# The rounded part of g written by GpSimd or by a casting transfer, and batch 3's squared rows added by GpSimd, in a fused channel attention and ELU feed-forward kernel

## The chip, the cores and the metric

The kernel runs on one core of a Trainium2 chip. The core has five engines that run at the same time, each with a queue of its own that it works through in order: TensorE (PE in the profile, with its weight loads as PEld), VectorE (DVE), ScalarE (ACT), GpSimd (POOL) and SyncE (SP, which here only starts transfers). Engines wait for one another through semaphores. Transfers run on 16 DMA engines. SBUF is the on-chip memory of 128 partitions, and PSUM is the memory that matmuls write to. The metric is the device time of one launch in microseconds; a time here is the median of its runs.

## The reference

Four batches (B) of 6080 rows (N) and 256 channels (C) go through a channel attention and then, as 24320 tokens, through a feed-forward layer of width 2048 with ELU:

```python
qn = q / (np.linalg.norm(q, axis=1, keepdims=True) + 1e-06)
kn = k / (np.linalg.norm(k, axis=1, keepdims=True) + 1e-06)
s = kn.transpose(0, 2, 1) @ qn / tau          # 256 x 256 for each batch
s = s - s.max(-1, keepdims=True)
a = np.exp(s)
a /= a.sum(-1, keepdims=True) + 1e-09
x = (v @ a).reshape(B * N, C)
h = x @ w_in                                  # 24320 x 2048
g = np.where(h > 0.0, h, np.exp(np.minimum(h, 0.0)) - 1.0)
out = g @ w_out                               # 24320 x 256
```

q, k, v are float32; the two weight matrices come as float64. The norms run over the 6080 rows.

## The kernel before, in words

The attention matrix of a batch is multiplied into `w_in` first, so that a batch has one matrix `wp` of 256 x 2048 and `h = v @ wp`. The tokens are cut into 12 chunks of 512 or 496 tokens for each batch, 48 chunks in all (`NCH`), and the feed-forward width into 16 blocks of 128 (`FT`). One step is one chunk `c` and one block `f`; there are 768 steps. The first four chunks share 64 steps in an interleaved order; from chunk 4 on, 16 steps in a row belong to one chunk.

Every matmul operand is kept as two parts: `hi`, the float32 value rounded to fp32r, and `lo`, what the rounding took away, also as fp32r. A product is then the sum of three fast matmuls: hi with hi, lo with hi, hi with lo. The helper `split` (L113 to L115) makes the two parts: ACT writes hi with a casting copy (L114) and DVE writes lo with a subtraction (L115).

`take(i)` (L833) issues step i:

- `h_item` (L416): six matmuls (L423, L424, L425, twice) of `wp` and the split chunk of v give `ph` in PSUM.
- `elu` (L428): gives `e`, of 128 x 512 float32 in SBUF. In even blocks ACT takes the exponential (L438), DVE limits it and subtracts one (L439) and takes the maximum with `ph` (L440). In odd blocks ACT does a Relu and an exponential (L434, L435) and DVE one combined instruction (L436). L439 has one input in SBUF; L436 and L440 have one in SBUF and one in PSUM.
- `split_g` (L443) of the step before: hi and lo of `e` go into a tile `g`.
- `out_item` (L455) of step i - 3 (`LAG`): six matmuls (L461, L463, L465, twice) add the product of g and `w_out` to `po`; L461 and L463 read hi, L465 reads lo. Between them stand single matmuls of the next batch's product of k and q (`gram_item`, L203 and L210).

There are three buffers for `e` and four for `g`. An `e` buffer is free again when its lo has been made, a `g` buffer when PE has used it.

Beside the steps run the next batch's rows: 24 groups of two rows in each partition are loaded by SP (`raw`, five buffers), squared by ACT (L181 into the single buffer `sq`), added to `acc` (L182, DVE, 128 x 1024 float32), and split for the gram matmuls (`qk`, L114 and L115). In the last group POOL first clears a part of the buffer (L169). Batch 1's groups run in chunks 4 to 10, batch 2's in chunks 13 to 21, batch 3's in chunks 25 to 33. After them come that batch's norms and softmax (L226 to L315) and its `wp` (L351 to L382), within the two chunks that follow. The chunks of v are split into hi and lo by L404 and L408. Both inputs lie in SBUF in the subtractions of L115 (g, qk) and L408 and in the additions of L182.

The order of PE, DVE and ACT is written out by hand up to step 66. After that a planner orders the instructions of each engine by the order in which they are traced and by the time at which it expects their inputs; `issue_after` keeps the work beside the steps behind the step's elu. The queues of SP and POOL are ordered by the planner as well.

Of the kernel before, what the change touches and what calls it, by code (L numbers as in the profile page):

```python
# [7 lines left out]
F32 = mybir.dt.float32  # L8
# [46 lines left out]
def channel_attention_then_elu_ffn(ctx: ExitStack, tc, q, k, vT, tau, w_in, w_out, outT):  # L55
# [8 lines left out]
    nc = tc.nc  # L64
    B, N, C = q.shape
# [9 lines left out]
    NB = len(sizes)  # L75
    NCH = B * NB
    LAG = 3


    M = 4  # L80
# [32 lines left out]
    def split(hi, lo, src):  # L113
        nc.scalar.copy(hi, src)  # L114
        nc.vector.tensor_sub(lo, src, hi.bitcast(F32))  # L115
# [50 lines left out]
    def load_rows(b, g):  # L166
        raw = work.tile([P, 2, 2, C], F32, tag="raw", bufs=5, name=f"raw_{b}_{g}")
        if 2 * g + 2 > RP:
            nc.gpsimd.memset(raw[:, :, 1, :], 0.0)  # L169
        fill_rows(raw, b, g)  # L170
        if 2 * g + 2 > RP:
            fill_left(raw, b)
        return raw

    def square_rows(raw, acc, first, sq=None):
        if first:
            nc.scalar.activation(acc, raw, AF.Square)
            return
        if sq is None:
            sq = work.tile([P, 2, 2, C], F32, tag="sq", bufs=1, name="sq")  # L180
        x = nc.scalar.activation(sq, raw, AF.Square)  # L181
        return x.ins, nc.vector.tensor_add(acc, acc, sq).ins  # L182

    def new_acc(b):
        return work.tile([P, 2, 2, C], F32, tag="acc", bufs=1, name=f"acc_{b}")

    def new_gram(b):
        return [ps.tile([P, 2, C], F32, tag="gram", bufs=KT, name=f"gram_{b}_{ct}") for ct in range(KT)]

    def split_rows(raw):  # L190
        hl = work.tile([P, 2, 2, 2, C], F32R, tag="qk", bufs=3, name="qk")
        split(hl[:, 0], hl[:, 1], raw)
        return hl

    def gram_item(hl, gram, ct, first, last):

        pg = gram[ct]  # L200
        cs = slice(ct * P, ct * P + P)
        for r in range(2):
            yield nc.tensor.matmul(  # L203
                pg,
                hl[:, 0, 1, r, cs],
                in_turns(hl[:, :, 0, r, :]),
                start=(first and r == 0),
                stop=False,
            )
            yield nc.tensor.matmul(  # L210
                pg[:, 0, :],
                hl[:, 1, 1, r, cs],
                in_turns(hl[:, 0, 0, r, :]),
                start=False,
                stop=(last and r == 1),
            )
# [53 lines left out]
    def norms(parts):  # L270

        pn = ps.tile([P, 2, C], F32, tag="w", bufs=WB, name="pn")
        for x in range(2):
            nc.tensor.matmul(pn[:, 0, :], ones_r, in_turns(parts[:, x, 0, :]), start=(x == 0), stop=(x == 1))
        for ct in range(KT):
            for x in range(2):

                nc.tensor.matmul(
                    pn[:, 1, 2 * ct : 2 * ct + 2],
                    parts[:, x, 1, ct * P : ct * P + P],  # L280
                    ones_r[:, 0:2],
                    start=(x == 0),
                    stop=(x == 1),
                )
        W = C + 2 * KT
        y, ry = (tiny.tile([P, W], F32, tag=x, bufs=1, name=x) for x in ("y", "ry"))
        nm = inverse_norms(y, ry, pn.rearrange("p x c -> p (x c)")[:, 0:W])
        rk = tiny.tile([P, 2 * KT], F32, bufs=2, tag="rk", name="rk")
        nc.vector.tensor_scalar(rk, ry[:, C:W], itau, None, op0=ALU.mult)

        return halves_of_turns(ry[:, 0:C]), rk.rearrange("p (c x) -> p c x", x=2)[:, :, 0], nm
# [26 lines left out]
    def soft_rows(b, gram):  # L318

        a = work.tile([P, KT, C], F32, tag="a", bufs=1, name=f"a_{b}")  # L320
        for ct in range(KT):
            row = halves(a[:, ct])
            nc.scalar.copy(row, halves_of_turns(gram[ct][:, 1, :]))
            nc.vector.tensor_add(row, halves_of_turns(gram[ct][:, 0, :]), row)
            if b == 1:
                nc.vector.tensor_add(a[:, ct], a[:, ct], state["early"][:, ct])
        return a
# [5 lines left out]
    def transpose_a(b, a):  # L333
        pt = ps.tile([P, KT, C], F32, tag="w", bufs=WB, name="pt")
        for jt in range(KT):
            for ct in range(KT):
                nc.tensor.transpose(pt[:, jt, ct * P : ct * P + P], a[:, ct, jt * P : jt * P + P], ident)  # L337
        if b == 0:
            aT = tiny.tile([P, KT, C], F32, tag="early", bufs=1, name=f"aT_{b}")
            for jt in range(KT):  # L340
                nc.scalar.copy(aT[:, jt], pt[:, jt])
            return aT
        aT = work.tile([P, 2, KT, C], F32R, tag="aT", bufs=1, name=f"aT_{b}")
        split(aT[:, 0], aT[:, 1], pt)
        return aT
# [12 lines left out]
    def new_wp(b):  # L358
        return [
            work.tile([P, 2, F], F32R, tag="wp", bufs=2 * KT, name=f"wp_{b}_{ct}") for ct in range(KT)  # L360
        ]
# [23 lines left out]
    def span(c):  # L385

        b, x = divmod(c, NB)
        return b, b * N + sum(sizes[:x]), sizes[x]
# [54 lines left out]
    def split_g(c, e):  # L443
        n = span(c)[2]
        g = work.tile([P, 2, CH], F32R, tag="g", bufs=4, name="g")
        split(g[:, 0, 0:n], g[:, 1, 0:n], e[:, 0:n])
        return g

    def first(c, f):
# [91 lines left out]
    acc = new_acc(0)  # L541
    pg0 = new_gram(0)
    wi64, wo64, vraw, vts = {}, {}, {}, {}
    state = {}
# [141 lines left out]
    def chunk_of(b):  # L686
        return b * NB
# [7 lines left out]
    def at(step, fn, free=False):  # L695
        (loose if free else side).setdefault(step, []).append(fn)
# [72 lines left out]
    def first_group(b):  # L769

        return EARLY if b == 1 else 0

    for b in range(1, B):
        s0 = M * FT if b == 1 else chunk_of(b - 1) * FT + FT
        s1 = chunk_of(b) * FT
        length = s1 - FT - 14 - s0

        g0 = first_group(b)

        def rows(b, g):  # L780
            if g == 0:
                state[b, "acc"], state[b, "gram"] = new_acc(b), new_gram(b)
            raw = state.pop((b, "raw", g))
            square_rows(raw, state[b, "acc"], g == 0)
            if g >= first_group(b):
                state[b, "hl", g] = split_rows(raw)

        def load(b, g):
            if g < NG:
                state[b, "raw", g] = load_rows(b, g)  # L790

        def gram(b, g, ct):
            g0 = first_group(b)
            yield from gram_item(state[b, "hl", g], state[b, "gram"], ct, g == g0, g == NG - 1)

        def soft_norms(b):
            state[b, "norms"] = norms(state[b, "parts"])
            state[b, "rs"] = tiny.tile([P, KT], F32, tag="sums", bufs=2, name="sums")

        def soft_sum(b):  # L800
            state[b, "a"] = soft_rows(b, state[b, "gram"])
            wps[b] = new_wp(b)

        def soft2(b):
            state[b, "aT"] = transpose_a(b, state[b, "a"])

        for g in range(NG):
            x = s0 + length * g // NG
            if g == 0:
                at(x, lambda b=b, g=g: (load(b, g), load(b, g + 1)))  # L810
            at(x + 2, lambda b=b, g=g: (rows(b, g), load(b, g + 2)))
            for ct in range(KT if g >= g0 else 0):
                fine[x + 5 + ct] = gram(b, g, ct)
        x = s1 - FT - 6
        at(x - 6, lambda b=b: state.__setitem__((b, "parts"), fold(state[b, "acc"])))
        at(x - 4, lambda b=b: soft_norms(b))
        at(x - 2, lambda b=b: soft_sum(b))
        for ct in range(KT):
            at(x + ct, lambda b=b, ct=ct: soft_exp(state[b, "a"], *state[b, "norms"], state[b, "rs"], ct))
        at(x + 3, lambda b=b: over_sums(state[b, "rs"]))  # L820
        at(x + 6, lambda b=b: soft2(b))
        x += 6
        for fq in range(FQ):
            at(x + 1 + 3 * fq, lambda b=b, fq=fq: state.__setitem__((b, "wi", fq), split_w_in(fq)))
            for ct in range(KT):
                at(x + 4 + 3 * fq + ct, lambda b=b, fq=fq, ct=ct: wp_item(state[b, "aT"], state[b, "rs"], state[b, "wi", fq], wps[b], ct, fq))
# [6 lines left out]
    def take(i):  # L833
# [5 lines left out]
        if 0 <= i - 1 < len(steps):  # L839
            gs[i - 1] = split_g(steps[i - 1][0], es.pop(i - 1))  # L840
        j = i - LAG
        if j >= 0:
# [16 lines left out]
    done = []  # L859
    for i in range(M * FT + LAG):  # L860
        take(i)
    in_order.close()
    for i in range(M * FT + LAG, len(steps) + LAG):
        take(i)
# [31 lines left out]
```

## Time and profile before

| | |
|---|---|
| median of the two timed runs | 2166.32 us (2165.83 and 2166.81) |
| span of the profiled execution, first to last instruction | 2163.4 us |
| instructions | 27196 |
| DMA | 120.77 MB, 56 GB/s on the mean |
| SP's issues of v, q, k, weights and out | all transfers but one, none by POOL |

The page lists no time of the profiled execution other than its span, so sums are made against the span; the timed runs lie 2.4 and 3.4 us above it. In the views, a row of instructions gives the line, the engine, the operation, what it writes and reads (out<-in), the count, then the busy time in us and the mean duration in ns, and last the idle time of the engine just before them with what ended it. A matmul's duration in the profile is longer than its spacing to the next, since matmuls are pipelined. L numbers are lines of the kernel before.

### The profile page before, as it was taken

Reading aid. Unit: us, or ns where it says so; the run is one execution under the profiler, and the core shown is the slowest. Engines: PE = TensorE matmul, PEld = TensorE weight load, DVE = VectorE, ACT = ScalarE, POOL = GpSimd, SP = SyncE. Lnnn points to the kernel's source line nnn. Section 1 sums busy time; section 2 is a strip of 40 time slices with the busy share of each in tenths; the row PEclk is TensorE's granted clock in tenths of the full one; section 3 lists DMA queues with packets and bytes.
Section 4 is the critical chain, followed back from the end, with each engine's and each line's share of the span. In section 5 each row is a group of like instructions: output and inputs, shape, how many; then the busy total and the mean of one; then the engine's idle time right before and its main releaser. Section 6 shows DMA issues by size and latency. Waiting matters only on the chain.

```text
span 2163.4 us, 27196 instructions
## 1 busy us (share of the span) xinstructions
PE 2158.6 (100%) x10240; PEld 1911.9 (88%) x10240; DVE 1527.0 (71%) x2358; ACT 1469.1 (68%) x2422; POOL 3.3 (0%) x11
## 2 busy tenths in 40 slices
PE   9999999999999999999999999999999999999999
PEld 8888888899888888889988888888998888888998
DVE  7987777778766776776776677667776666666665
ACT  6877777667666666666766666666776666666665
POOL 0000000000000000000000000000000000000000
PEclk9999999999999999999999999999999999999999
DMA  9320222221111111111111112111112000000000
GB/s 357 107 78 30 78 69 68 68 65 49 59 38 50 49 59 49 59 58 46 39 59 39 49 50 68 49 58 49 56 31 67 20 30 27 23 20 11 20 10 20
DMA packets 62532, 120.77 MB, mean 56 GB/s; under 512 B 6208, under 2 KB 16064, under 8 KB 62400
## 3 DMA queue, kind: packets, MB, share of 16 engines
q1 hardware_dynamic: 62256, 118.91, 16.6%
q8 instruction: 80, 1.31, 0.2%
q14 instruction: 52, 0.43, 0.1%
q10 hardware_dynamic: 144, 0.13, 0.0%
HBM read 92.01 MB, written 27.00 MB: 55 GB/s over the span
## 4 chain that ended last, share of the span: by engine, by line
PE 100%; ACT 0%; DVE 0%; issue 0%
PE po L465 15%; PE po L463 15%; PE ph L423 15%; PE po L461 15%; PE ph L424 15%; PE ph L425 15%; PE gram L203 3%; PE gram L549 2%; PE gram L210 1%; PE pw L374 1%; PE pw L373 1%; PE pw L375 1%; PE pe L549 0%; PE pw L370 0%; PE pd L222 0%; PE pt L337 0%
## 5 line engine op out<-in xcount | busy, mean ns | idle before, releaser
L114 ACT CAST g<-e 128x512 fp32r<-128x512 f32 (+1 forms) x768 | 469.6, 611 | 483.5 <-DVE e L440 281.6
L115 DVE TENSOR_TENSOR g<-e,g 128x512 fp32r<-128x512 f32 (+1 forms) x768 | 525.6, 685 | 323.0 <-ACT g L114 295.6
L465 PE MATMUL po<-g,wo 128*128 128x512 f32 (+1 forms) x1536 | 579.3, 377 | 0.0
L463 PE MATMUL po<-g,wo 128*128 128x512 f32 (+1 forms) x1536 | 579.2, 377 | 0.0
L461 PE MATMUL po<-g,wo 128*128 128x512 f32 (+1 forms) x1536 | 578.9, 377 | 0.0
L423 PE MATMUL ph<-vt,wp 128*128 128x512 f32 (+1 forms) x1472 | 555.4, 377 | 0.0
L425 PE MATMUL ph<-vt,wp 128*128 128x512 f32 (+1 forms) x1472 | 554.5, 377 | 0.0
L424 PE MATMUL ph<-vt,wp 128*128 128x512 f32 (+1 forms) x1472 | 554.5, 377 | 0.0
L436 DVE SCALAR_TENSOR_TENSOR e<-e,ph 128x512 f32<-128x512 f32 (+1 forms) x416 | 283.2, 681 | 242.5 <-ACT e L435 241.9
L434 ACT ACTIVATE e<-ph 128x512 f32<-128x512 f32 (+1 forms) x416 | 246.6, 593 | 129.1 <-PE ph L425 114.4
L461 PEld LDWEIGHTS po<-g,wo 128*128 128x128 f32 x1536 | 290.3, 189 | 37.9 <-DVE scr L478 0.2
L463 PEld LDWEIGHTS po<-g,wo 128*128 128x128 f32 x1536 | 290.3, 189 | 37.8
L465 PEld LDWEIGHTS po<-g,wo 128*128 128x128 f32 x1536 | 290.7, 189 | 34.8 <-DVE g L115 0.3
L424 PEld LDWEIGHTS ph<-vt,wp 128*128 128x128 f32 x1472 | 278.2, 189 | 36.2
L425 PEld LDWEIGHTS ph<-vt,wp 128*128 128x128 f32 x1472 | 278.2, 189 | 36.1
L423 PEld LDWEIGHTS ph<-vt,wp 128*128 128x128 f32 x1472 | 278.2, 189 | 36.1
L435 ACT ACTIVATE e<-e 128x512 f32<-128x512 f32 (+1 forms) x416 | 261.3, 628 | 12.6
L440 DVE TENSOR_TENSOR e<-ph,e 128x512 f32<-128x512 f32 (+1 forms) x352 | 240.6, 684 | 10.4
L438 ACT ACTIVATE e<-ph 128x512 f32<-128x512 f32 (+1 forms) x352 | 207.9, 591 | 31.1 <-PE ph L425 29.2
L439 DVE TENSOR_SCALAR e<-e 128x512 f32<-128x512 f32 (+1 forms) x352 | 147.0, 418 | 20.7 <-ACT e L438 20.6
L182 DVE TENSOR_TENSOR acc<-acc,sq 128x1024 f32<-128x1024 f32 x84 | 102.6, 1221 | 12.2 <-ACT sq L181 11.1
L203 PE MATMUL gram<-qk 128*128 128x512 f32 x268 | 101.6, 379 | 0.0
(134 smaller groups left out, 1183.1 us busy)
## 6 DMA issues: line engine op xcount, KB each, us to landing
raw<-in_q_dram SPq DMA_DIRECT2D x76, 256.0 KB, 2.7
raw<-in_k_dram SPq DMA_DIRECT2D x76, 256.0 KB, 3.0
v<-in_v_dram SPq DMA_DIRECT2D x32, 512.0 KB, 3.6
out_dram<-o SPq DMA_DIRECT2D x56, 256.0 KB, 2.1
v<-in_v_dram SPq DMA_DIRECT2D x16, 496.0 KB, 3.5
out_dram<-o SPq DMA_DIRECT2D x31, 248.0 KB, 2.1
wraw<-w_scr SPq DMA_DIRECT2D x12, 512.0 KB, 3.2
room<-in_q_dram SPq DMA_DIRECT2D x16, 256.0 KB, 5.2
```

What stands on the lines that cost most here:

```text
L114: nc.scalar.copy(hi, src)
L115: nc.vector.tensor_sub(lo, src, hi.bitcast(F32))
L423: nc.tensor.matmul(ph[:, 0:n], wp[kt][:, 0, fs], hi, start=(kt == 0), stop=False)
L424: nc.tensor.matmul(ph[:, 0:n], wp[kt][:, 0, fs], lo, start=False, stop=False)
L425: nc.tensor.matmul(ph[:, 0:n], wp[kt][:, 1, fs], hi, start=False, stop=(kt == KT - 1))
L434: nc.scalar.activation(ev, pv, AF.Relu, scale=-1.0)
L435: x = nc.scalar.activation(ev, ev, AF.Exp, scale=-1.0)
L436: y = nc.vector.scalar_tensor_tensor(ev, ev, -1.0, pv, op0=ALU.add, op1=ALU.max)
L440: y = nc.vector.tensor_tensor(ev, pv, ev, op=ALU.max)
L461: nc.tensor.matmul(o, wo[:, f, 0, ds], hi, start=first(c, f), stop=False)
L463: nc.tensor.matmul(o, wo[:, f, 1, ds], hi, start=False, stop=False)
L465: nc.tensor.matmul(o, wo[:, f, 0, ds], lo, start=False, stop=last(c, f))
```

## The change

Three things change.

In chunks 8 to 15 (`POOL_COPIES`) hi is written by GpSimd's copy in place of ScalarE's. In chunks 20 to 27 (`POOL_CASTS`) it is written by a transfer from SBUF to SBUF, started from GpSimd's queue, that casts float32 to fp32r. In the other chunks ScalarE writes it as before. lo stays with VectorE everywhere. The squared rows of batch 3 are added to `acc` by GpSimd; those of batches 1 and 2 stay with VectorE. 128 steps are touched by the copies, 128 by the casts, and 23 additions move.

```diff
+    POOL_COPIES, POOL_CASTS = (8, 16), (20, 28)
...
-    def square_rows(raw, acc, first, sq=None):
+    def square_rows(raw, acc, first, sq=None, adder=nc.vector):
...
         x = nc.scalar.activation(sq, raw, AF.Square)
-        return x.ins, nc.vector.tensor_add(acc, acc, sq).ins
+        return x.ins, adder.tensor_add(acc, acc, sq).ins
...
         g = work.tile([P, 2, CH], F32R, tag="g", bufs=4, name="g")
-        split(g[:, 0, 0:n], g[:, 1, 0:n], e[:, 0:n])
+        hi, lo, src = g[:, 0, 0:n], g[:, 1, 0:n], e[:, 0:n]
+        if POOL_COPIES[0] <= c < POOL_COPIES[1]:
+            nc.gpsimd.tensor_copy(hi, src)
+        elif POOL_CASTS[0] <= c < POOL_CASTS[1]:
+            nc.gpsimd.dma_start(hi, src)
+        else:
+            nc.scalar.copy(hi, src)
+        nc.vector.tensor_sub(lo, src, hi.bitcast(F32))
         return g
...
-            square_rows(raw, state[b, "acc"], g == 0)
+            square_rows(raw, state[b, "acc"], g == 0, None, nc.gpsimd if b == B - 1 else nc.vector)
```

## The prediction, made before the changed kernel was built or run

> **What bounds the kernel now.** I read the page first (busy times, the clock row, the chain that ended last), then the waits, then the stretches in which the changed chunks run, then single instructions in order of time.
>
> ```profile
> span 2163.4 us, 27196 instructions
> ...
> PE 2158.6 (100%) x10240; PEld 1911.9 (88%) x10240; DVE 1527.0 (71%) x2358; ACT 1469.1 (68%) x2422; POOL 3.3 (0%) x11
> ...
> PEclk9999999999999999999999999999999999999999
> ...
> PE 100%; ACT 0%; DVE 0%; issue 0%
> ```
>
> TensorE (PE) is busy for all but 4.8 us of the span, at the full clock, and the chain that ended last is PE alone. So no work taken off ScalarE (ACT) or VectorE (DVE) can shorten the span by more than those 4.8 us, and they lie at its two ends. The change takes no matmul away. It can cost nothing or make PE wait. The question is how much room lies between the moment g is finished and the moment PE needs it. Of all the weight loads of the out product, one waited for g:
>
> ```profile
> PEld po L465 <- DVE g L115: 0.3, 1, 0.3
> ```
>
> The room of an ordinary step shows in the timeline of chunk 9 (start, duration, engine, line):
>
> ```profile
> 504.33 0.67 DVE L440 TENSOR_TENSOR e<-ph,e 128x496 f32<-128x496 f32 x1
> ...
> 505.03 0.61 ACT L114 CAST g<-e 128x496 fp32r<-128x496 f32 x1 [0.18 <-DVE e L440]
> ...
> 505.67 0.67 DVE L115 TENSOR_TENSOR g<-e,g 128x496 fp32r<-128x496 f32 x1 [0.67 <-ACT g L114]
> ...
> 509.74 0.37 PE L461 MATMUL po<-g,wo 128*128 128x496 f32 x1
> ...
> 510.49 0.38 PE L465 MATMUL po<-g,wo 128*128 128x496 f32 x1
> ```
>
> e is ready at 505.00, the rounded part (hi) at 505.64, the rest (lo) at 506.34. PE takes hi at 509.74 and lo at 510.49. Both are 4.1 us early. Where a batch's norms and softmax run, the room is nearly gone; in chunk 10 a lo that ends at 530.90 is loaded at 531.36:
>
> ```profile
> 530.23 0.67 DVE L115 TENSOR_TENSOR g<-e,g 128x496 fp32r<-128x496 f32 x1
> ...
> 531.36 0.19 PEld L465 LDWEIGHTS po<-g,wo 128*128 128x128 f32 x1
> ```
>
> The stretches in question are 418.7 to 778.4 us (chunks 8 to 15, the copies) and 957.7 to 1313.4 us (chunks 20 to 27, the casts). Columns: length, then busy time and count of PE, PEld, DVE, ACT, POOL, clock, DMA share, GB/s.
>
> ```profile
> 418.70:778.40 359.70, 359.70 (x1728) 320.37 (x1728) 257.94 (x402) 245.99 (x409) 0.68 (x1) 1.00 0.16 52
> 957.70:1313.40 355.70, 355.70 (x1703) 316.69 (x1703) 251.03 (x394) 241.30 (x403) 0.73 (x1) 1.00 0.15 48
> ```
>
> PE has no hole in either, and GpSimd (POOL) is idle.
>
> **The change, part 1: 128 copies move from ACT to POOL (chunks 8 to 15).** What ACT loses:
>
> ```profile
> L114 ACT CAST g<-e 128x512 fp32r<-128x512 f32 (+1 forms) x128 | 78.2, 611 | 80.2 <-DVE e L440 42.7 <-DVE e L436 37.3
> ```
>
> These 78.2 us buy nothing, since ACT bounds nothing. What POOL takes for such a copy, before does not show. The nearest rows (mean ns of one):
>
> ```profile
> L169 POOL MEMSET raw<- 128x512 f32 x3 | 2.1, 715 | 1516.7 <-DVE qk L115 1516.7
> L559 POOL MEMSET ragged<- 128x512 f32 x1 | 0.5, 528 | 0.0
> masks.py:199 POOL TENSOR_SCALAR_AFFINE_SELECT ident<-ident 128x128 f32<-128x128 f32 x1 | 0.3, 293 | 0.0
> ```
>
> The lower end is 0.53 us, the undisturbed memset of the same shape. The select, the one POOL row that also reads, gives 4 x 0.293 = 1.17 us for four times the elements. If a casting copy reads and writes in turn instead of together, it is 1.17 + 0.72 = 1.89 us, the upper end. I take 1.85, near the upper end: I count on the slow case of reading, rounding and storing in one pass per element each, and this is the weakest step of the sum. As a delay alone it is harmless: 1.85 - 0.61 = 1.24 us against 4.1.
>
> What matters more is whether POOL and DVE can work at once. The memset ran beside DVE three times; the first:
>
> ```profile
> 457.74 0.41 DVE L439 TENSOR_SCALAR e<-e 128x496 f32<-128x496 f32 x1
> ...
> 457.94 0.68 POOL L169 MEMSET raw<- 128x512 f32 x1 [456.18 <-DVE qk L115]
> ...
> 458.07 0.67 DVE L115 TENSOR_TENSOR g<-e,g 128x496 fp32r<-128x496 f32 x1
> ```
>
> It took 0.68 us where the undisturbed one took 0.53, longer by 0.15, and it had met the last 0.21 us of the tensor_scalar. The subtraction that followed kept its usual 0.67 us beside it. So one kind of DVE instruction (one input, at double rate: 417 ns where two inputs take 682) keeps POOL out, and a write alone does not hinder a subtraction. The copy reads as well as writes. I take it that it and DVE's instructions with two SBUF inputs exclude each other in the same way. The Trainium skill states this (SBUF — State Buffer, "Who interferes with whom"): the two share one pair of ports, a two-input DVE instruction contends with a GpSimd instruction that reads and not with one that only writes, and the second to start waits for the whole first. The three rows agree with both halves they can show; no row shows a POOL read beside DVE, and by the rule the sum below stands, without it part 1 is near nothing.
>
> DVE's instructions in the copies' stretch:
>
> ```profile
> L115 DVE TENSOR_TENSOR g<-e,g 128x512 fp32r<-128x512 f32 (+1 forms) x128 | 87.3, 682 | 57.3 <-ACT g L114 56.0
> L440 DVE TENSOR_TENSOR e<-ph,e 128x512 f32<-128x512 f32 (+1 forms) x64 | 43.6, 681 | 1.8
> L436 DVE SCALAR_TENSOR_TENSOR e<-e,ph 128x496 f32<-128x496 f32 (+1 forms) x64 | 43.3, 677 | 35.7 <-ACT e L435 35.7
> L439 DVE TENSOR_SCALAR e<-e 128x512 f32<-128x512 f32 (+1 forms) x64 | 26.7, 417 | 2.3 <-ACT e L438 2.3
> L182 DVE TENSOR_TENSOR acc<-acc,sq 128x1024 f32<-128x1024 f32 x16 | 19.5, 1221 | 2.2 <-ACT sq L181 2.2
> L115 DVE TENSOR_TENSOR qk<-raw,qk 128x1024 fp32r<-128x1024 f32 x16 | 19.5, 1218 | 1.7 <-ACT qk L114 1.7
> L408 DVE TENSOR_TENSOR vt<-v,vt 128x512 fp32r<-128x512 f32 (+1 forms) x16 | 10.8, 676 | 0.0
> ```
>
> The five groups that have two SBUF inputs or the double rate come to 87.3 + 26.7 + 19.5 + 19.5 + 10.8 = 163.8 us; L436 and L440 have one of their inputs in PSUM and are taken as free of POOL. The copies add 128 x 1.85 = 236.8. Together 400.6 us must pass one after the other in 359.7 us: at least 41 us over. The break-even of a copy is (359.7 - 163.8) / 128 = 1.53 us. Packing will not be perfect: the next copy needs the next e, which DVE makes in L436 or L440 (43.6 + 43.3 = 86.9 us) behind a blocked subtraction in its queue. If half of that finds POOL idle, the excess is 41 + 43 = 84; if DVE and POOL strictly alternate it is 257.9 + 236.8 - 359.7 = 135. I take the middle of 41 and 84: +63 us. Queued behind a blocked subtraction on DVE are the next e, the split of v and qk and so, three steps later, PE.
>
> **Part 2: 128 rounded parts come by a casting transfer (chunks 20 to 27).** ACT loses about as much again, for nothing. POOL issues 128 transfers of 256 KB from SBUF to SBUF. Before has none of these; the nearest by size (KB each, us from issue to landing):
>
> ```profile
> raw<-in_k_dram SPq DMA_DIRECT2D x76, 256.0 KB, 3.0
> out_dram<-o SPq DMA_DIRECT2D x56, 256.0 KB, 2.1
> room<-in_q_dram SPq DMA_DIRECT2D x16, 256.0 KB, 5.2
> ```
>
> So 2.1 us with free queues, 5.2 among the crowd of the start. The DMA engines are 0.15 busy here, so I take 3.0 and 0.5 for POOL's own issue (as long as its memset): 3.5, later than ACT by 2.9. An ordinary step has 4.1 to spare and loses nothing. In batch 2's softmax (chunk 22), where the spare is 0.5 as in chunk 10, a step comes 2.4 late. The lateness moves PE and so gives room to the next: 2.4 at least, 25 if some ten steps each pay in full. I take +10. The subtraction waits for the transfer at the head of DVE's queue, where the next step's e stands behind it; this too fits as long as the transfer takes under two steps (355.7 / 128 = 2.78 each). SP's queue loses and gains nothing; its loads share the DMA engines. The two memsets of POOL (L169 in chunks 8 and 20) now stand among copies and casts; each waits for a free raw buffer, and if put early holds those behind it by up to a step or so: taken as nothing, at most 6 us.
>
> **Part 3: batch 3's additions go to POOL.** DVE loses the 23 of the first row; 8 (second row) fall in the casts' chunks 25 to 27.
>
> ```profile
> L182 DVE TENSOR_TENSOR acc<-acc,sq 128x1024 f32<-128x1024 f32 x23 | 28.1, 1220 | 3.1 <-ACT sq L181 3.1
> ...
> L182 DVE TENSOR_TENSOR acc<-acc,sq 128x1024 f32<-128x1024 f32 x8 | 9.7, 1215 | 0.0
> ```
>
> On POOL such an addition is between the memset's rate (8 x 128 elements, about 1.0 us) and the select's (8 x 0.293 = 2.3). At 2.3 it is hidden by the 4.1 us and by the 17 us between two of them (8 in the 134.8 us of chunks 25 to 27); with that cover gone it is 23 x (2.3 - 1.2) = 25. A cast issued behind one of the eight is up to 2.3 later, 5.8 in all against 4.7 of room: +1 each at worst, half of them: +4.
>
> **Sum.** 63 + 10 + 4 = 77 us on the profiled execution's 2163.4 us of span; the two timed runs lie about 3 us above that span (median 2166.3). 2166.3 + 77 = 2243 us.
>
> **The rivals.** (1) Not slower: the copy is short, or does not exclude DVE. With 1.36 us (select rate plus one 0.19 wait, the memset's 0.72 - 0.53) POOL and DVE need 163.8 + 174 = 338 us of 359.7 and the 4.1 us absorb the rest. Only parts 2 and 3 remain: 2166 to 2185, some 2178. It decides below 1.53 us a copy. For it speaks the select's 1.17, against it that the cast must read, round and write a full stream. The Trainium skill (GPSIMD Engine Reference, section 4.1) calls one-input work on this engine roughly line-rate, which would put the copy under 0.8 us and the sum at this rival's. (2) The casts are the trouble: landings over 4.7 us. e has three buffers and PE runs three steps behind, so each step pays a third of what is over: at 5.2 us 128 x 0.17 = 21, at 7 us 128 x 0.77 = 98, with part 1 small: 2190 to 2270. The rows with free queues speak against it. (3) Faster: PE's 4.8 us of not being busy is all there is, under 2%.
>
> **How the numbers follow.** The forecast's mechanism (POOL and DVE exclude each other and the copy is over 1.53 us) has 0.58, own range 2205 to 2320; rival 1 0.32; rival 2 0.08; faster 0.02. A measurement tells about 2% (43 us) from no change: the forecast is over that except in its lowest part (0.02), rival 2 mostly. So faster 0.02, same 0.35, slower 0.63. The range leaves out the strict alternation with late casts and the exact tie: 2168 to 2315.
>
> **What would show it.** Right: in the copies' stretch POOL's copies take about 1.85 us each, PE has holes that end with L115 (lo) or a copy, the stretch grows from 360 to about 420 us, and DVE's subtractions stand idle behind POOL rather than run longer. Wrong: copies under 1.5 us, or copies and subtractions that overlap in time without loss. For part 2: casts landing in about 3.5 us and the stretch longer by 5 to 20 us only around the softmax; for part 3: no hole in PE after 1360 us. The prediction fails most easily on the copy's duration, next on whether a copy excludes a subtraction.

## The result, and the profile after

The changed kernel takes 2186.39 us (median of two runs, 2184.45 and 2188.34) where the kernel before takes 2166.32: a ratio of 1.0095, with a 95% interval of 1.0078 to 1.0111. The change costs 20 us, under the 2% that count as slower. The forecast was 2243.

The page of the changed kernel (part 1, the chain's shares, the transfers' row: count, KB each, median us from issue to landing):

```profile
span 2182.5 us, 27584 instructions
...
PE 2167.3 (99%) x10240; PEld 1910.4 (88%) x10240; DVE 1528.3 (70%) x2335; ACT 1326.7 (61%) x2166; POOL 220.6 (10%) x290
...
PE 33%; ACT 3%; DVE 3%; issue 1%; DMA 0%; DVEq 0%
...
g<-e POOLq DMA_DIRECT2D x64, 256.0 KB, 2.3
```

The chain that was PE alone now passes through ACT and DVE, and its shares add up to 40%: beyond that it could not be followed back. Stretches by the same steps as before (the windows' columns are those of the prediction: length, busy time and count of PE, PEld, DVE, ACT, POOL, clock, DMA share, GB/s):

```profile
418.70:779.30 360.60, 360.52 (x1728) 320.01 (x1728) 264.38 (x402) 179.09 (x283) 92.98 (x127) 1.00 0.17 52
958.90:1331.20 372.30, 362.76 (x1703) 315.98 (x1702) 243.84 (x388) 171.97 (x275) 85.21 (x134) 1.00 0.43 134
```

The copies' stretch took 359.7 us and takes 360.6, with PE busy throughout. The casts' stretch took 355.7 and takes 372.3: 16.6 of the 19.1 us by which the span grew. What PE's weight loads waited for in the whole run (us in total, times, longest us):

```profile
PEld po L469 <- DMA g<-e: 10.1, 10, 2.5
PEld po L473 <- DVE g L454: 6.4, 14, 1.0
PEld ph L424 <- DVE wp L383: 2.9, 3, 1.2
```

L469 loads hi, L473 lo (L461 and L465 before), L454 is the subtraction, L449 the copy, L451 the cast. PE waits for casts and for what follows a cast on DVE; no row names the copy. The copies' stretch by lines:

```profile
L449 POOL CAST g<-e 128x512 fp32r<-128x512 f32 (+1 forms) x126 | 92.3, 732 | 260.0 <-DVE e L441 122.8 <-DVE e L437 117.0 <-PE po L473 9.9
L454 DVE TENSOR_TENSOR g<-e,g 128x512 fp32r<-128x512 f32 (+1 forms) x128 | 88.0, 688 | 76.9 <-POOL g L449 75.5 <-ACT g L453 1.4
...
L183 DVE TENSOR_TENSOR acc<-acc,sq 128x1024 f32<-128x1024 f32 x16 | 22.5, 1406 | 1.8 <-ACT sq L182 1.7
L116 DVE TENSOR_TENSOR qk<-raw,qk 128x1024 fp32r<-128x1024 f32 x16 | 22.3, 1395 | 0.0
```

A copy takes 0.73 us on the mean, not 1.85. Beside it DVE's long instructions with two SBUF inputs take 1.41 and 1.40 us instead of 1.22 each: something is exclusive, but little.

### The profile page after: what moved, and what is told of

Same layout as the page of the kernel before. It is cut to its first block, busy times and chain, and to the rows that moved or that the text cites. A ratio compares the mean times of both kernels' runs of the same rounds, so it can differ in the third digit from the quotient of the medians.

```text
span 2182.5 us, 27584 instructions
## 1 busy us (share of the span) xinstructions
PE 2167.3 (99%) x10240; PEld 1910.4 (88%) x10240; DVE 1528.3 (70%) x2335; ACT 1326.7 (61%) x2166; POOL 220.6 (10%) x290
## 5 line engine op out<-in xcount | busy, mean ns | idle before, releaser
L454 DVE TENSOR_TENSOR g<-e,g 128x512 fp32r<-128x512 f32 (+1 forms) x768 | 531.6, 693 | 403.2 <-ACT g L453 193.6
L469 PE MATMUL po<-g,wo 128*128 128x512 f32 (+1 forms) x1536 | 580.2, 378 | 6.3 <-DMA g<-e 6.3
L473 PE MATMUL po<-g,wo 128*128 128x512 f32 (+1 forms) x1536 | 581.1, 378 | 1.8 <-DVE g L454 1.4
L453 ACT CAST g<-e 128x512 fp32r<-128x512 f32 (+1 forms) x512 | 313.4, 612 | 352.3 <-DVE e L441 217.6
L437 DVE SCALAR_TENSOR_TENSOR e<-e,ph 128x512 f32<-128x512 f32 (+1 forms) x416 | 283.1, 681 | 172.8 <-ACT e L436 171.7
L469 PEld LDWEIGHTS po<-g,wo 128*128 128x128 f32 x1536 | 290.3, 189 | 47.7 <-DMA g<-e 10.1
L473 PEld LDWEIGHTS po<-g,wo 128*128 128x128 f32 x1536 | 290.8, 189 | 40.9 <-DVE g L454 6.4
L441 DVE TENSOR_TENSOR e<-ph,e 128x512 f32<-128x512 f32 (+1 forms) x352 | 240.7, 684 | 10.3
L440 DVE TENSOR_SCALAR e<-e 128x512 f32<-128x512 f32 (+1 forms) x352 | 147.9, 420 | 20.6 <-ACT e L439 20.1
L449 POOL CAST g<-e 128x496 fp32r<-128x496 f32 (+1 forms) x128 | 93.5, 730 | 673.8 <-ACT e L435 412.4
L116 DVE TENSOR_TENSOR qk<-raw,qk 128x1024 fp32r<-128x1024 f32 x67 | 105.0, 1568 | 18.6 <-ACT qk L115 17.2
```

Of the source, the lines that this page charges most:

```text
L437: y = nc.vector.scalar_tensor_tensor(ev, ev, -1.0, pv, op0=ALU.add, op1=ALU.max)
L441: y = nc.vector.tensor_tensor(ev, pv, ev, op=ALU.max)
L469: nc.tensor.matmul(o, wo[:, f, 0, ds], hi, start=first(c, f), stop=False)
L473: nc.tensor.matmul(o, wo[:, f, 0, ds], lo, start=False, stop=last(c, f))
```

## The experiments

Times are medians, in us. The kernel before took 2165.6 to 2166.0 in every one of these comparisons.

| run | what differs | us | ratio, interval |
|---|---|---|---|
| e1_copies | copies alone | 2166.47 | 1.0004, 0.9994 to 1.0013 |
| e2_casts | casts alone | 2177.56 | 1.0055, 1.0038 to 1.0072 |
| e3_adds | additions alone | 2166.93 | 1.0005, 0.9995 to 1.0014 |
| e11_copies_twice | each copy made twice | 2209.64 | 1.0203, 1.0188 to 1.0219 |
| e4_copies_thrice | each copy made three times | 2251.76 | 1.0398, 1.0382 to 1.0413 |
| e14_twice_later | twice, lo behind the next e | 2168.04 | 1.0011, 1.0001 to 1.0021 |
| e13_thrice_later | three times, lo behind the next e | 2184.68 | 1.0088, 1.0070 to 1.0106 |
| e12_copies_for_casts | additions, and copies in chunks 20 to 27 | 2168.10 | 1.0012, 1.0002 to 1.0021 |
| e5_casts_quiet | casts alone, in chunks 38 to 45 | 2169.41 | 1.0017, 1.0007 to 1.0026 |
| e6_casts_quiet_loads | the same with loads added | 2170.60 | 1.0023, 1.0014 to 1.0033 |
| e10_casts_late_adds | casts, additions only behind them | 2178.14 | 1.0058, 1.0043 to 1.0073 |
| e9_before_lag4 | before, PE four steps behind | 2167.60 | 1.0009, 0.9999 to 1.0018 |
| e7_lag4 | the whole change, four steps | 2180.22 | 1.0066, 1.0051 to 1.0081 |
| e15_lag4_later | e7, lo behind the next e | 2177.45 | 1.0053, 1.0036 to 1.0069 |
| e16_later | the whole change, lo behind the next e | 2190.72 | 1.0113, 1.0097 to 1.0128 |
| e17_lag4_no_adds | e7 without the additions | 2173.97 | 1.0037, 1.0024 to 1.0051 |
| e18_lag4_later_no_adds | e15 without the additions | 2170.66 | 1.0023, 1.0013 to 1.0033 |
| e19_later_no_adds | e16 without the additions | 2177.36 | 1.0053, 1.0038 to 1.0068 |

### One part at a time

```diff
-    POOL_COPIES, POOL_CASTS = (8, 16), (20, 28)
+    POOL_COPIES, POOL_CASTS = (8, 16), (48, 48)   # e1; e2 (48, 48), (20, 28); e3 both (48, 48)
...
-            square_rows(raw, state[b, "acc"], g == 0, None, nc.gpsimd if b == B - 1 else nc.vector)
+            square_rows(raw, state[b, "acc"], g == 0, None, nc.vector)    # e1 and e2
```

> The copies alone (chunks 8 to 15), no casts, batch 3's additions on DVE. Theory A (a copy takes 0.73 us in the mean, under the 1.53 us at which POOL and DVE would fill the stretch, so they are free; the loss lies with the casts): 0 to 2 us over before. Rival B (the exclusion of POOL and DVE makes the loss, in the copies' stretch too, and shows later as a shifted queue): 5 us or more.

> The casts alone (chunks 20 to 27), batch 3's additions on DVE. Theory A (casts that land late because other transfers are in flight): 10 to 15 us over before, the rest of the 19 us of span being casts that stand behind an addition on POOL. Rival B (POOL's additions make the loss): under 5 us. Rival C (the planner's other order of the queues makes it, whatever the casts do): about 17 us, as in the changed kernel.

> Batch 3's additions alone on POOL, ACT makes every rounded part. Theory A: 0 to 2 us over before, since a subtraction that is held for up to 1.8 us has 4.1 us of room. Rival B (the exclusion makes the loss): 5 us or more.

The copies cost 0.5 us, the additions 1.0, neither of them apart from nothing by its interval; the casts cost 11.6. The three make 13.1, the whole change 20.1. So 7 us come only when parts are together, and the term of 63 us is gone.

### Why the copies cost nothing, and when they would

```diff
-            nc.gpsimd.tensor_copy(hi, src)
+            for _ in range(3):                        # e4; range(2) in e11
+                nc.gpsimd.tensor_copy(hi, src)
```

> As the copies alone, but POOL makes each copy three times over, 3 x 0.62 = 1.85 us without waiting, which is the duration that the prediction took. If POOL and DVE really exclude each other as the prediction has it, 163.8 + 128 x 1.85 = 400 us have to pass in 360 us: 40 to 85 us over before. If they only delay each other a little, the added delay of 1.24 us is within the 4.1 us of room: 0 to 5 us over before.

> As the copies alone, but each made twice, 2 x 0.62 = 1.24 us, under the break-even of 1.53 us. If the exclusion of POOL and DVE is what cost 86 us with three copies: 163.8 + 128 x 1.24 = 322 us fit into 360, and the time is 0 to 15 us over before. If it was the delay of the copy (its cost growing by the same amount with each copy): 40 us or more.

A copy that waits for nothing takes 0.62 us, so three hold POOL for about the 1.85 us of the prediction, and they cost 86 us, within the 41 to 135 of its part 1. But two, 1.24 us and under its break-even of 1.53, cost 44: the second copy costs about 43 and the third 42, and no threshold shows. A part of this may be clock: the granted clock of the stretch was 0.97 in e4 and 0.99 in e11, and if matmuls lengthen with it, 359.7 us of them grow by 11 and 4 us, an estimate; how much of that PE would have waited anyway is not separated. The timeline of e11 (start, us, engine, line; x1 is a single copy, x2 the two copies of a step; L455 is the subtraction there):

```profile
654.61 0.62 POOL L450 CAST g<-e 128x512 fp32r<-128x512 f32 x1
...
655.87 0.68 DVE L437 SCALAR_TENSOR_TENSOR e<-e,ph 128x512 f32<-128x512 f32 x1
...
656.68 1.29 POOL L450 CAST g<-e 128x512 fp32r<-128x512 f32 x2 [1.46 <-DVE e L437]
658.01 0.69 DVE L455 TENSOR_TENSOR g<-e,g 128x512 fp32r<-128x512 f32 x1 [1.46 <-POOL g L450]
...
658.62 0.42 DVE L440 TENSOR_SCALAR e<-e 128x512 f32<-128x512 f32 x1
...
659.08 0.69 DVE L441 TENSOR_TENSOR e<-ph,e 128x512 f32<-128x512 f32 x1
```

The reader is to see that POOL and DVE take turns although nothing but the order asks for it: DVE makes an e (L437), has that e's subtraction next in its queue, and stands 1.46 us at it while POOL copies. Behind it stand L440 and L441, which make the next e, and POOL has nothing to copy until they have. If order is the cause, the loss should go when the subtraction is put behind the next e, with the same work on both engines:

```diff
-            gs[i - 1] = split_g(steps[i - 1][0], es.pop(i - 1))
+            c = steps[i - 1][0]
+            with tc.issue_after(done[1].ins) if POOL_COPIES[0] <= c < POOL_COPIES[1] else ExitStack():
+                gs[i - 1] = split_g(c, es.pop(i - 1))
```

> The same with two copies (1.24 us). Theory E (the order on DVE): 0 to 6 us over before, where the two copies with the planner's own order cost 44 us. Theory F (exclusion, with a lower break-even than the 1.53 us worked out): 30 us or more.

> Three copies for each rounded part as before (1.85 us), but in the copies' chunks the subtraction that makes lo stands behind the next step's e on DVE's queue, so that DVE does not wait for the copies of the step that it has just finished. Theory E (what cost 86 us was the order on DVE: e, then a wait for POOL, then lo, then the next e, which leaves DVE idle while POOL copies): 0 to 25 us over before. Theory F (POOL and DVE exclude each other and together have more than the stretch holds, 400 us in 360): 41 us or more over before.

It goes: two copies cost 2.3 us in place of 44, three cost 19 in place of 86. The same place of the timeline in e14:

```profile
642.45 0.69 DVE L437 SCALAR_TENSOR_TENSOR e<-e,ph 128x512 f32<-128x512 f32 x1 [1.14 <-ACT e L436]
643.05 0.68 DVE L455 TENSOR_TENSOR g<-e,g 128x512 fp32r<-128x512 f32 x1
643.27 1.63 POOL L450 CAST g<-e 128x512 fp32r<-128x512 f32 x2 [0.80 <-DVE e L437]
...
644.37 0.81 DVE L440 TENSOR_SCALAR e<-e 128x512 f32<-128x512 f32 x1 [0.63 <-ACT e L439]
```

Here L455 is the subtraction of the step before, and DVE goes on while POOL copies. The pair that starts into it takes 1.63 us instead of 1.29, so the exclusion is there. Nor are the three e buffers the limit, since here the subtraction, which frees a buffer, comes later behind its e than in e11 (3.0 us, there 2.2) and the loss is gone.

With three copies the exclusion also bounds less than was thought: 3 x 0.62 x 128 = 238 us and DVE's 163.8 are the prediction's 400 in 359.7 again, at least 41 over by its sum, and 19 were measured. All five groups do exclude a copy: in e13 (418.7 to 798 us) the subtractions of g, vt and qk take 0.82, 1.08 and 1.62 us on the mean, the additions 1.62 and L440 0.71, where before had 0.68, 0.68, 1.22, 1.22 and 0.42; L441 and L437, with one input in PSUM, keep 0.68 and 0.67. But part of each record lies beside the other engine's without harm. L440 above starts beside the second copy and ends 0.28 us after the pair, though it takes 0.42 alone. In e13 a copy and one of these instructions follow each other in this way 360 times, and each time the second ends 0.14 to 0.15 us sooner than its own time behind the first would have it: 53 us in all. That takes the sum from 402 to 349 us, under the 359.7, so the two engines' work by itself does not fill the stretch. What PE waits for in e13 is mostly a lo that comes late:

```profile
PEld po L474 <- DVE g L455: 13.5, 17, 1.5
```

The Trainium skill (GPSIMD Engine Reference, section 4.1) calls one-input work on this engine roughly line-rate; 0.62 us against ACT's 0.61 for the same copy agrees with it, and the select, from which the prediction scaled, was no measure of a copy.

### Where a cast costs

```diff
-    POOL_COPIES, POOL_CASTS = (8, 16), (20, 28)
+    POOL_COPIES, POOL_CASTS = (48, 48), (38, 46)      # e5, e6; additions on VectorE
...
+    def dummy(n):                                     # e6
+        raw = work.tile([P, 2, 2, C], F32, tag="raw", bufs=5, name=f"dummy_{n}")
+        fill_rows(raw, B - 1, n % (NG - 1))
+
+    for n, i in enumerate(range(38 * FT, 46 * FT, 6)):
+        at(i, lambda n=n: dummy(n))
...
+    POOL_COPIES, POOL_CASTS = (20, 28), (48, 48)      # e12; additions on GpSimd
```

e6 brings two loads of 256 KB every six steps, which nothing reads.

> 128 casts as in the change, but in chunks 38 to 45, where SP loads only v and stores the output, with no rows of a next batch and no softmax; batch 3's additions on DVE. Theory A (casts are late where other transfers are in flight or where the room is small): 0 to 4 us over before. Rival C (a cast is too late by itself, or the planner's order is): 10 us or more.

> As the casts in chunks 38 to 45, with one more group of rows loaded (two transfers of 256 KB on SP, not used) every six steps, as often as the rows of a batch come; the additional loads are no part of the reference's work. Theory A: some 22 casts land one to two microseconds later than without the loads, and the time is 3 to 10 us over that of the casts without them. If sharing the DMA engines is not the cause: within 1 us of it.

> POOL copies in place of the casts in chunks 20 to 27, with batch 3's additions on POOL as in the change. If the casts make the loss: 0 to 4 us over before. If those chunks cannot bear POOL's work (softmax, additions): 10 us or more.

The same 128 casts cost 3.8 us in chunks without a next batch and 11.6 in their own; copies in that place, with the additions, cost 2.3. So it is neither the place nor the casts by themselves but both. Added loads brought 1.2 us, inside the two intervals' overlap: mere traffic of that size explains little. What the place adds is a smaller room. In the trace of before, lo is at least 4.2 us ahead of the weight load that needs it in every step of chunks 38 to 45; in chunks 20 to 27 it is less than 4 us ahead in 29 of the 128 steps, and 0.4 at the least. Late landings alone do not do it: 22 casts of e6 landed more than 3 us after their issue, 26 of e2, and e6 lost less than half as much. The transfers of the changed kernel around its worst cast (DMA view of ten microseconds; issues with count, KB, median us to landing):

```profile
q8 instruction: 1, 0.02, 0.6%
...
g<-e POOLq DMA_DIRECT2D x3, 248.0 KB, 4.8
v<-in_v_dram SPq DMA_DIRECT2D x1, 512.0 KB, 4.3
out_dram<-o SPq DMA_DIRECT2D x2, 248.0 KB, 4.7
```

and its timeline there:

```profile
1091.37 0.53 POOL L451 DMA_DIRECT2D g<-e  x1 [2.47 <-PE ph L426]
...
1097.60 0.19 PEld L469 LDWEIGHTS po<-g,wo 128*128 128x128 f32 x1 [0.78 <-DMA g<-e]
1097.60 0.48 PE L469 MATMUL po<-g,wo 128*128 128x496 f32 x1 [0.39 <-DMA g<-e]
```

The cast issued at 1091.37 shares the engines with a load of v and two stores and is taken up by PE 6.2 us later. Single meetings of this kind, and not the mean traffic, fit what the spacing of PE's steps shows: a few steps lose 1 to 3 us each and most lose nothing. In the changed kernel's trace the 64 casts with no packet of another queue in flight beside them all landed 2.18 to 2.36 us after their issue; the 27 that took over 3 us are all among the other 64. No run moved a load away from a cast, so that the meeting delays the cast stays a reading. In e5 two casts landed late with no other transfer near, only one packet of the instruction queue:

```profile
q0 software_dynamic: 288, 0.52, 36.6%
q8 instruction: 1, 0.02, 1.9%
issues: line engine op xcount, KB each, median us to landing
g<-e POOLq DMA_DIRECT2D x2, 256.0 KB, 3.4
```

They landed 3.7 and 3.1 us after issue where 2.2 is usual. Of the 30 casts of e5 that met such packets and nothing else, 7 took over 3 us; of the 77 that met nothing, none did. That the fetch of instructions delayed them is read off the overlap; no run took it away.

### Casts behind additions

```diff
-            square_rows(raw, state[b, "acc"], g == 0, None, nc.gpsimd if b == B - 1 else nc.vector)
+            square_rows(raw, state[b, "acc"], g == 0, None, nc.gpsimd if b == B - 1 and g >= 8 else nc.vector)
```

> Casts in chunks 20 to 27 as in the change; of batch 3's additions only those from the ninth group on (after chunk 27) go to POOL, so that none stands among the casts. If the 7 us between the casts alone (11.6 us over before) with the additions alone (1.0) and the whole change (20) come from casts that wait behind an addition on POOL and subtractions that wait for one on DVE: 11 to 14 us over before. If the two parts cost more together for another reason: 17 us or more.

e10 has the casts and no copies. With only the additions that come behind the last cast, the loss is 12.4 us, that of the casts alone. So the further 7 us belong to the eight additions among the casts. One of them in the changed kernel:

```profile
1240.15 0.69 DVE L441 TENSOR_TENSOR e<-ph,e 128x512 f32<-128x512 f32 x1
...
1240.86 2.37 POOL L183 TENSOR_TENSOR acc<-acc,sq 128x1024 f32<-128x1024 f32 x1
...
1242.62 1.17 DVE L454 TENSOR_TENSOR g<-e,g 128x512 fp32r<-128x512 f32 x1 [1.78 <-DMA g<-e]
1243.16 0.57 POOL L451 DMA_DIRECT2D g<-e  x1
1243.71 1.21 DVE L116 TENSOR_TENSOR qk<-raw,qk 128x1024 fp32r<-128x1024 f32 x1
1243.84 0.19 PEld L473 LDWEIGHTS po<-g,wo 128*128 128x128 f32 x1 [0.97 <-DVE g L454]
```

The cast behind the addition is issued at 1243.16 though its e was ready at 1240.8, and the subtraction that starts beside the addition takes 1.17 us instead of 0.69 and ends 0.56 us after the addition. Two delays meet in steps that the casts have already left without room.

### Room and order

Two remedies were tried on the whole change: PE four steps behind instead of three (with a fifth buffer for g, paid for by letting another tile share a buffer), and the casts' subtraction behind the next e, as had helped the copies.

```diff
-    LAG = 3
+    LAG = 4                                           # e7, e9, e15, e17, e18
...
+        def low():
+            nc.vector.tensor_sub(lo, src, hi.bitcast(F32))
+
+        if POOL_CASTS[0] <= c < POOL_CASTS[1]:            # e15, e16, e18, e19
+            later.append(low)
...
+        if later:                                         # behind the next step's elu
+            with tc.issue_after(done[1].ins):
+                later.pop()()
```

> The whole change, with g used four steps after it is begun instead of three and five buffers for g (the place comes from a tile of the weights' conversion that now shares another's). Theory A (lateness over the room, which grows by one step, 2.7 us): PE has hardly a hole in the casts' stretch, and the time is within 5 us of the same kernel without the change. Rival D (DVE's queue itself, blocked at its head, or e's three buffers are the limit): still 10 us or more over it.

> The kernel before with g used four steps later and five buffers for g: the control for the changed kernel with the same edit. Every theory: the time of before within 4 us, since PE waits for nothing there; one step more at the end costs PE nothing but a longer tail of at most 3 us.

> The whole change with PE four steps behind and five buffers for g, and in the casts' chunks the subtraction of a step is put on VectorE behind the next step's e instead of ahead of it. Theory (what the casts still cost with four steps of room, 12.6 us over the kernel before in that arrangement, is VectorE standing at a subtraction that waits for a late transfer, with the next e, wp's and qk's subtractions queued behind it): under 5 us over the kernel before with four steps, 2167 to 2172 us, and PE's waits for wp L383 and qk L116, 5.5 and 4.4 us, shrink to about 1 each. Rival (the transfers' own lateness or the traffic is what is left): 10 us or more still over it, 2177 to 2181.

> The whole change with PE three steps behind as it is, and only the casts' subtraction put behind the next step's e. Theory (VectorE's order is a good part of the loss, the room of PE the other): clearly less than the change's 20 us, some 5 to 12 over the kernel before, 2171 to 2178, with PE's waits for the cast itself (10.1 us at its weight loads) now the larger part of what is left. Rival (order is nothing, the room alone): 17 to 25 over, 2183 to 2191, since lo comes one addition later and the room is the same.

A step more of room leaves 12.6 us over its own control (2180.22 - 2167.60), and PE's waits in e7 move from the casts to what lies behind them in DVE's queue:

```profile
PEld ph L424 <- DVE wp L383: 5.5, 4, 2.1
PEld gram L204 <- DVE qk L116: 4.4, 5, 1.4
...
PEld po L469 <- DMA g<-e: 0.7, 2, 0.4
```

This spoke for the order of DVE's queue. But the later subtraction, which was to take most of the 12.6, left 9.9, and with three steps it made the change no better, 24.8 over before against 20. The theory that VectorE's order is what the casts cost fell, and the trace of e16 shows what had been left out:

```profile
1222.74 0.69 DVE L441 TENSOR_TENSOR e<-ph,e 128x512 f32<-128x512 f32 x1
...
1223.28 2.35 POOL L183 TENSOR_TENSOR acc<-acc,sq 128x1024 f32<-128x1024 f32 x1 [1.25 <-ACT sq L182]
1223.35 2.83 DVE L457 TENSOR_TENSOR g<-e,g 128x512 fp32r<-128x512 f32 x1
...
1225.59 0.57 POOL L453 DMA_DIRECT2D g<-e  x1
...
1226.24 0.19 PEld L481 LDWEIGHTS po<-g,wo 128*128 128x128 f32 x1 [2.08 <-DVE g L457]
```

A subtraction that begins 0.07 us behind POOL's addition takes 2.83 us instead of 0.68: it ends 0.55 us after the addition, so that all but 0.13 us of its own work came behind it, and its whole record counts as busy. PE waits 2.08 us for it. By the spacing of PE's steps, six additions in a row cost 1.95 us each. The Trainium skill (SBUF — State Buffer, "Who interferes with whom") says that the one that issues first keeps the shared ports for its whole instruction and the other is fully blocked; for the addition this trace agrees, but for those last 0.13 us. So the last three runs take only the additions away:

> PE four steps behind, copies and casts as in the change, batch 3's additions back on VectorE. Theory (what is left with four steps of room is for the larger half GpSimd's additions, each of 2.4 us, standing ahead of a cast and shutting VectorE's subtraction out): the change's 2180.2 us in this arrangement fall by 5 to 7, to 2173 to 2175. Rival (the casts' own lateness is nearly all): at most 2 us less, 2178 to 2181.

> The same with the casts' subtraction behind the next e. Theory (additions): 2177.4 us fall by about 6, to 2170 to 2173, some 5 us over the kernel before, since in that run chunks 26, 27 and 30 held 6.3 us of the loss, each at a subtraction that began beside an addition. Rival: 2176 to 2178.

> PE three steps behind, the casts' subtraction behind the next e, additions on VectorE. Theory (additions): in the run with the additions on GpSimd the chunks 25 to 27 lost 15 us, 1.95 at each of six additions, where the subtraction began beside the addition and took 2.83 us; these go: 2190.7 falls by 12 to 15, to 2176 to 2179. Rival (the later subtraction costs by itself, since it takes PE's room): at most 5 less, 2186 to 2190.

They bring 6.3, 6.8 and 13.4 us. The subtractions of chunks 25 to 27, first in e16:

```profile
L457 DVE TENSOR_TENSOR g<-e,g 128x512 fp32r<-128x512 f32 x48 | 45.7, 952 | 0.9 <-DMA g<-e 0.7
```

then in e19:

```profile
L457 DVE TENSOR_TENSOR g<-e,g 128x512 fp32r<-128x512 f32 x52 | 35.6, 684 | 1.1 <-DMA g<-e 0.8
```

Their mean falls by 0.268 us, 48 of them by 12.9, about the 13.4 gained. What is left without additions is the casts' lateness: 11.6 and 11.7 us with three steps, whichever way VectorE is ordered (e2, e19), and 6.4 and 3.1 over the control with four (e17, e18). All runs of e18 lie below those of e17 (2171.0 at most, 2172.3 at least), but the two intervals overlap, so an effect of the order there is likely and not shown. No run is faster than the kernel before.

## Why the prediction was right or wrong

**Size: wrong.** It gave the mechanism of 77 us a chance of 0.58; measured were 20, within 2%. The result lies in the range, near its low end, and 1.4 us above the 2166 to 2185 of rival 1, which had 0.32. That it lies in the range is luck: the largest term, 63 us, came to 0.5.

**The step that failed** is the copy's price: "I take 1.85, near the upper end". Measured is 0.73 with its waits and 0.62 without, near the lower end, the memset's 0.53. The rate of the select was scaled up to a copy, and rounding was supposed to cost a pass of its own. With that the 63 us of part 1 fall to 0.5.

**The sum behind it failed too,** though nobody would see it in this change alone. The break-even of 1.53 us and the "at least 41" were drawn from adding up two engines that exclude each other. Two copies cost 44 us below that threshold and, in another order, 2.3; three cost 19, below the floor, because 53 us of the records lay side by side. Most of the price was not in the ports but in DVE's queue, where the subtraction stood ahead of the next e. The prediction named that as "packing" and gave it 43 us for half; it is nearly the whole of the 44 with two copies and 67 of the 86 with three.

**Exclusion itself: right.** It shows in DVE's 1.41 and 1.40 us beside copies and in the 2.83 beside an addition.

**Casts: the term right, its reasons half.** +10 was said, 11.6 measured for casts alone. A cast is issued 0.53 us after its e is ready and lands 2.3 us after that by the median: some 2.8 in all, under the 3.5 taken. The stretch did not lose "only around the softmax" but in single steps from chunk 20 to 27, and chunk 22, where the prediction put the loss, lost nothing in the changed kernel's trace. 27 of the 128 casts landed 3.0 to 6.2 us after issue, two of them beyond the 4.7 us of rival 2's condition. So that 10 came near 11.6 is partly luck.

**Additions: duration right, place right, price too small.** 2.3 us was taken, 2.38 measured:

```profile
L183 POOL TENSOR_TENSOR acc<-acc,sq 128x1024 f32<-128x1024 f32 x23 | 54.7, 2380 | 224.2 <-ACT sq L182 224.0
```

Alone they cost 1.0 us, and in the changed kernel one step near 1491 us is 0.9 longer, where the prediction saw no hole. Among the casts they cost 7 and not 4: it counted the later cast but not the shut-out subtraction. In chunks 28 to 33, without casts, the same exclusion is all but harmless: the qk subtractions of 1331 to 1700 us take twice their 1.22 us and PE has the room for it:

```profile
L116 DVE TENSOR_TENSOR qk<-raw,qk 128x1024 fp32r<-128x1024 f32 x16 | 40.1, 2506 | 18.0 <-ACT qk L115 16.7 <-DMA wraw<-w_scr 1.3
```

## What to carry to other kernels

Scale the duration of an unseen instruction from a row of the same kind, and where two rows lie far apart let the one with the same shape count; here the memset of that shape was off by 0.1 us and the scaled select by a factor of two. Adding up the records of two engines that exclude each other is too strict by what the records overlap without harm, here 0.14 us at each turn; what a wait costs is said by what stands behind the waiting instruction in its queue. Two delays that are each harmless, a late transfer and a blocked subtraction, are no longer so in the same step: ask of each whether the other has already used the room.

## What the runs showed of the hardware that was not expected

- A GpSimd casting copy of 128x512 takes 0.62 us undisturbed, as long as ScalarE's 0.61.
- DVE's subtraction behind a GpSimd addition waits for all but its last 0.13 us (2.83 us for 0.68), and its record shows this as busy time, not as idle time: 952 ns on the mean in place of 684 was the sign.
- A casting transfer of 256 KB within SBUF begins to be issued 0.53 us after its source is ready, takes GpSimd 0.53 us, and lands 2.2 to 2.3 us after the issue begins. The Trainium skill (DMA: Bandwidth & Descriptors, "Anatomy of one DMA — SWDGE (gpsimd) path") fits the transfers that GpSimd issues by 2.0 us and 436 GB/s, an estimate of 2.6 us for 256 KB; the trace has somewhat less.
- A GpSimd copy and a DVE instruction with two SBUF inputs, or L440, exclude each other, but the second to start ends 0.14 to 0.15 us sooner than behind the first's whole record (360 times in e13).
- In these traces casts land late only beside packets of other queues: none of 64 without them took over 2.36 us in the changed kernel, and 27 of 64 with them took over 3. Two in e5, 3.7 and 3.1 us, stood beside a single packet of the instruction queue, with no other queue's transfer in flight.
